# Feed-forward in eight blocks of 256 rows instead of four of 512: row-stationary gate and up, DMA transposes, queries in the first four units

## The chip, the cores and the metric

The kernel runs on one core of a Trainium2 chip. The metric is the device time of one launch in microseconds (us). Five engines matter: TensorE (PE in the profile, with its weight loads as PEld), VectorE (DVE), ScalarE (ACT), GpSimd (POOL) and SyncE, whose queue (SPq) issues nearly all DMAs.

## The reference

One transformer block on 2048 rows of width 512, with modulation vectors made from a condition `c`:

```python
x = A_x
mod = (_silu(c) @ w_mod).reshape(c.shape[0], 6, 1, -1)
sa, ca, ga, sb, cb, gb = (mod[:, 0], mod[:, 1], mod[:, 2], mod[:, 3], mod[:, 4], mod[:, 5])
h = _layernorm(x, axis=-1) * (1 + ca) + sa
x = x + ga * _A_ref(h, A_wq, A_wk, A_wv, A_wo)      # 32 heads of 16, one shared key and value head
h = _layernorm(x, axis=-1) * (1 + cb) + sb
x = x + gb * _B_ref(h, B_w_gate, B_w_up, B_w_down)  # (sigmoid(h Wg) * (h Wu)) Wd, inner width 1792
```

`_A_ref` is softmax attention over all 2048 keys. All inputs and the output are fp32.

## The kernel before

**Precision.** Every projection is made of three fp16 products: an fp32 operand is split into a high half and a low remainder, and high·high, low·high and high·low are added in PSUM. So each output tile of 128 rows and 512 columns costs three matmuls for every 128 of inner width.

**Attention.** The main loop runs over 32 units: eight query chunks of 256 rows (`NQ`), four groups of eight heads each (`NU`). A unit has 16 steps (`NKB`), one for each 128 keys. In a step PE makes four `sa` tiles (scores with queries on the partitions), whose row maxima DVE takes (`mx`), for units further on: these run 84 tiles ahead. It makes four `st` tiles (scores transposed, with the maximum already subtracted through extra rows of the query operand), which ACT turns into `P` by an exponential, and the products of `P` with `V` into the bank `craw`. At the end of a unit ACT copies `craw` into `cs`, a few small DMAs (`lD`, `raw`, `lc`) reorder it, and POOL makes the attention output `a` of that unit. All these matmuls use half the array's rows and a quarter of its columns each (64*32 in the profile); the helper `columns` issues four beside each other.

**Filling with feed-forward.** PE's spare time in each half step is filled by `piece`, which takes the next portion of a queue of groups: the query projections (`q`), the output projection (`wo`), gate and up (`gu`), down (`dn`). A `Couple` runs two groups on the upper and lower 64 rows of the array at once, so that one portion is eight 64*32 matmuls. `pick` chooses the next group, `places` spreads it over half steps at a rate (`RATE` 2.2 portions a half step, `QRATE` 0.55 for early queries, at most `MOST`). `pinned` order is kept: what the loop emits is each engine's program order.

**Blocks.** The feed-forward works on blocks of 512 rows (`QB`, four of them). When the eight units of a block are done, its four `wo` groups (128 rows each) are made in two Couples, then `norm`, `norm2` and `normed` (add to `x`, layer norm, on DVE and POOL), then PE transposes the normalised rows (`tr_part`, bank `pt`), and `split_evac` lets ACT scale and shift them and POOL split them into `h2h` and `h2l`, width on the partitions. For each of 14 chunks of 128 inner columns the weight chunk `gw` (512 KB, split halves kept in DRAM as `wD`) is stationary and the 512 rows of `h2` move: the gate bank goes through ACT (`th`, a tanh), the up bank through DVE (`u`), and POOL makes `gh` and `gl`, which already lie with inner width on the partitions, as `down_group` needs them.

**Tail.** The last block's attention ends with the loop, so its feed-forward runs alone, as full 128*128 matmuls (`alone`, line 187): the four down groups that `KEPT` left over, then transposes, 14 chunks of gate and up, and down.

**Weights** are loaded, scaled and split by `split_weight` during the first units (`WSTEPS`, `WLAST`); `w_down`'s first rows share their place with the query weights and come last. SP issues all DMAs from one queue in program order; a DMA there waits for its data and then the next one is reached. `defer(n, f)` emits `f` n steps later.

The lines with which the prediction works:

```python
def norm2(t, t1, xr):
    row_norm([t1], [xr], later=True)
    defer(1, lambda: normed(t, t1, xr))
...
gs += [Couple(gu_group(p, 0, at + p), gu_group(p, 1, at + p)) for p in range(max(lo, ahead), hi)]
gs += [Couple(down_group(t, lo), down_group(t + 1, lo)) for t in (0, 2)]
```

Of the kernel before, what the change touches and what calls it, by code (L numbers as in the profile page):

```python
# [16 lines left out]
P = 128  # L17
# [4 lines left out]
F = 1792  # L22
# [42 lines left out]
KEPT = 2  # L65
RATE = 2.2
QRATE = 0.55
ERATE = 1.2
AHEAD = 0, 0, 0, 0
MOST = 3  # L70
SWAP = 5
FRESH = 0.9
WSTEPS = 110
WLAST = 175
WLATE = 2
WSTORE = 5
FIRST = 140
# [7 lines left out]
GWB = 4  # L85
HBUFS = 36
# [3 lines left out]
def adaln_mqa_glu_kernel(  # L90
# [133 lines left out]
    def t16(name):  # L224
        return wp.tile([P, 512], F16, tag="f16", name=name, bufs=HBUFS)
# [76 lines left out]
    MCOLS = {1: ("ca", 1.0, SH), 0: ("sa", 0.0, SH), 4: ("sc", 1.0, SH), 3: ("sh", 0.0, SH)}  # L302
    MROWS = {2: ("ga", 1.0 / SW), 5: ("gb", 1.0 / (2.0 * SH * SW * SW))}

    def mod_end(i):
        p_ = mods[i]
        if i in MCOLS:
            name, add, mul = MCOLS[i]
            mods[i] = cp.tile([P, NDC], F32, name=name)
            dve.tensor_scalar(mods[i], p_[:, :NDC], add, mul, op0=ALU.add, op1=ALU.mult)  # L310
        else:
            name, scale = MROWS[i]
            mods[i] = cp.tile([P, D], F32, name=name)
            act.activation(mods[i], p_, AF.Identity, scale=scale)
# [38 lines left out]

    def split_evac(src, k, sc, sh, hi, lo):
        h32 = t32("h32")[:, :QU]
        act.activation(h32, src, AF.Identity, scale=sc[:, k:k + 1], bias=sh[:, k:k + 1])
        pool.tensor_scalar(hi, h32, 1.0, 0.0, op0=ALU.mult, op1=ALU.add)  # L357
        pool.tensor_tensor(lo, h32, hi, op=ALU.subtract)

# [93 lines left out]
    def ln1_high(b, k):  # L453
        hh, hl = h1.setdefault(b, ([], []))
        hh.append(t16(f"h1h{k}"))
        hl.append(t16(f"h1l{k}"))
        act.activation(hh[k], pts[b, k], AF.Identity, scale=mods[1][:, k:k + 1], bias=mods[0][:, k:k + 1])
# [24 lines left out]
    def k_high(b):  # L482
        pks[b, "h"] = kh = t16("kh")
        act.activation(kh, pks[b], AF.Identity, scale=kscale, bias=kbias)
# [22 lines left out]
    def q_group(b, o):  # L507
# [5 lines left out]
        def end(pq, second):  # L513
            qdone.add((b, o))
            q2 = wp.tile([P, 2, 512], F16, tag="q2", name="q2", bufs=2)
# [195 lines left out]
    def finish(b, o, raw):  # L711
        a_ = t16("a")
# [18 lines left out]
    def last_unit():  # L731
# [8 lines left out]
        a_ = t16("a")  # L740
# [14 lines left out]
    wD = dr.tile([NFC, P, 4, NDC, P], F16, name="wD")  # L755

    def gw_tile():
        return P2.tile([P, 4, NDC, P], F16, tag="gw", name="gw", bufs=GWB)

    def weight_jobs():
# [3 lines left out]
        def gate_up(f, m):  # L766
            if m == 0:
                gw[f] = gw_tile()
            split_weight((w_gate, w_up)[m][:, f * P:(f + 1) * P].rearrange("(k p) n -> p k n", p=P),
                         gw[f][:, 2 * m], gw[f][:, 2 * m + 1], [NDC, P],  # L770
                         (lambda: sp1.dma_start(wD[f], gw.pop(f))) if m == 1 else None)
# [3 lines left out]
        for f in [*range(4, NFC), *range(4)]:  # L775
            for m in range(2):
                jobs.append(lambda f=f, m=m: gate_up(f, m))
        for k in [*range(4, NFC), *range(4)]:
# [8 lines left out]
    class Transposes:  # L787
        stage, n = "tr", 4

        def __init__(self, part, u, sizes):  # L790
            self.part, self.u, self.sizes = part, u, sizes

        def alone(self):
            self.part(0, 4)

    def ffn_groups(b):
        x1 = {}
        xrs = {}
        h2 = {}
        gT = {}  # L800
        gws = {}
        ths = {}
        fs = [*range(4, NFC), *range(4)]
        HF = 8
        ahead = 2 * AHEAD[b]
        uses = [(p, 0) for p in range(ahead)]
        uses += [(p, None) for p in range(NFC)]
        asked = [0]

        def wo_group(t):  # L810
            def term(n, rs):
                o, i = divmod(n, 3)
                a_, w_ = passes(*aTs[2 * b + t // 2, o], WO['woh'], WO['wol'])[i]
                return a_[rs, t % 2 * P:(t % 2 + 1) * P], w_[rs, o, :]

            def begin():
                xrs[t] = t32("xr")
                sp1.dma_start(xrs[t], x[b * QB + t * P:b * QB + (t + 1) * P, :])

            def end(po, second):  # L820
# [6 lines left out]
                if tail:  # L827
                    dve.tensor_tensor(xr, t1, xr, op=ALU.add)
                    row_norm([t1], [xr])
                    normed(t, t1, xr)  # L830
                else:
                    defer(1 + 2 * (t % 2), lambda: norm(t, t1, xr))

            return Group("wo", 12, "po", term, end, begin)

# [9 lines left out]
        def normed(t, t1, xr):  # L845
            x1[t] = (xr, t1)
            if t % 2 == 1:
                marks[b, t // 2] = now[0]
            if t == (1 if ahead else 3):
                ask(2 if ahead else GWB - 1)  # L850

        pts2 = {}

        def tr_part(u, z, n0, n1):
            if n0 == 0:
                pts2[z] = bank("pt2")
            pt = pts2[z]
            for n in range(n0, n1):
                k, t = 2 * z + n // 2, 2 * u + n % 2
                pe.transpose(pt[:, n * P:(n + 1) * P], x1[t][1][:, k * P:(k + 1) * P], ident)  # L860
            if n1 == 4:
                for k in range(2 * z, 2 * z + 2):
                    if u == 0:
                        h2[k] = t16("h2h"), t16("h2l")
                    split_evac(pt[:, k % 2 * QU:(k % 2 + 1) * QU], k, mods[4], mods[3],
                               *(h_[:, u * QU:(u + 1) * QU] for h_ in h2[k]))

        def ask(upto):
            while asked[0] < min(upto, len(uses)):
                k = asked[0]  # L870
                gws[k] = gw_tile()
                sp1.dma_start(gws[k], wD[fs[uses[k][0]]])
                asked[0] += 1

        def parts_of(p):
            if p not in gT:
                gT[p] = t16("gh"), t16("gl")
            return gT[p]

        def gu_half(p, m, u, at):  # L880
            us = slice(u * QU, (u + 1) * QU)

            def term(n, rs):
                e, (k, i) = n // 12, divmod(n % 12, 3)
                gw = gws[at + e]
                w_, h_ = passes(gw[:, 2 * m], gw[:, 2 * m + 1], *h2[k])[i]
                return w_[rs, k, :], h_[rs, us], lambda z: z[:, e * QU:(e + 1) * QU]

            def end(p_, second):
                gated(p, m, p_, second, [(e, us, slice(e * QU, (e + 1) * QU)) for e in range(2)])  # L890

            return Group("gu", 24, "pgu", term, end, (lambda: ask(at + GWB)) if m == 0 else None, w=0.5)

        def gated(p, m, p_, second, pieces):
            if m == 0:
                ths[p] = th = t32("th")
                act.activation(th, p_, AF.Tanh, scale=0.5 / (SH * SW))  # L897
                return
            th = ths.pop(p)
            if second:  # L900
                u_ = t32("u")
                dve.tensor_copy(u_, p_)
                pool.tensor_scalar(th, th, 1.0, 1.0, op0=ALU.add, op1=ALU.mult)  # L903
                pool.tensor_tensor(th, th, u_, op=ALU.mult)
            else:
                dve.scalar_tensor_tensor(th, th, 1.0, p_, op0=ALU.add, op1=ALU.mult)  # L906
            for e, to, of in pieces:
                hi, lo = parts_of(fs[p + e])
                pool.tensor_scalar(hi[:, to], th[:, of], 1.0, 0.0, op0=ALU.mult, op1=ALU.add)
                pool.tensor_tensor(lo[:, to], th[:, of], hi[:, to], op=ALU.subtract)  # L910

        def gu_group(p, m, at):
            def term(n, rs):
                k, i = divmod(n, 3)
                gw = gws[at]
                w_, h_ = passes(gw[:, 2 * m], gw[:, 2 * m + 1], *h2[k])[i]
                return w_[rs, k, :], h_[rs]

            def end(p_, second):
                gated(p, m, p_, second, [(0, slice(0, QB), slice(0, QB))])  # L920

            return Group("gu", 12, "pgu", term, end, (lambda: ask(at + GWB)) if m == 0 else None)

        def down_group(t, lo):
            n_ = HF if lo == 0 else NFC - HF

            def term(n, rs):
                f, i = fs[lo + n // 3], n % 3
                g_, w_ = passes(*gT[f], wdh, wdl)[i]
                return g_[rs, t * P:(t + 1) * P], w_[rs, f, :]  # L930

            def end(p_, second):
# [8 lines left out]
                else:  # L941
                    pool.tensor_tensor(ot, ot, x1[t][0], op=ALU.add)
                    store = lambda: sp1.dma_start(out[b * QB + t * P:b * QB + (t + 1) * P, :], ot)
                    if tail:
                        store()
                    else:
                        defer(2 + t % 2, store)
# [3 lines left out]
        wos = [wo_group(t) for t in range(4)]  # L951
        trs = [Transposes(lambda n0, n1, u=u, z=z: tr_part(u, z, n0, n1), u, ([4], [4, 0])[z]) for z in range(2) for u in range(2)]
        gs = []
        at = len(uses) - NFC
        es = [Couple(gu_half(p, 0, 0, p), gu_half(p, 1, 0, p)) for p in range(0, ahead, 2)]
        gs += [Couple(gu_half(p, 0, 1, at + p), gu_half(p, 1, 1, at + p)) for p in range(0, ahead, 2)]
        for lo, hi in ((0, HF), (HF, NFC)):
# [263 lines left out]
```

## Time and profile before

| | |
|---|---|
| median of 3 runs | 1664.54 us (1663.61 to 1665.8) |
| span of the profiled execution | 1661.5 us |
| mean granted TensorE clock | 0.994 |
| PE / DVE / ACT / POOL busy, share of the span | 98% / 85% / 78% / 38% |
| DMA | 94.06 MB, mean 57 GB/s |
| first copy of `craw` (unit 0 ends) / last (unit 31 ends) | 153.4 / 1524.4 us |

The profiled execution's own time is its span of 1661.5 us and the launch around it; the median of the timed runs stands 3.0 us above that span. Units can be told apart in the trace by ACT's 32 copies `cs<-craw`, one at the end of each. A matmul's duration in the profile includes the way through the array, so 379 ns stands beside starts that are 0.22 us apart; rates are read from starts, or from counts over a stretch, not from durations.

### The profile page before, as it was taken

Reading aid. Unit: us, or ns where it says so; the run is one execution under the profiler, and the core shown is the slowest. Engines: PE = TensorE matmul, PEld = TensorE weight load, DVE = VectorE, ACT = ScalarE, POOL = GpSimd, SP = SyncE. Lnnn points to the kernel's source line nnn. Section 1 sums busy time; section 2 is a strip of 40 time slices with the busy share of each in tenths; the row PEclk is TensorE's granted clock in tenths of the full one; section 3 lists DMA queues with packets and bytes.
Section 4 is the critical chain, followed back from the end, with each engine's and each line's share of the span. In section 5 each row is a group of like instructions: output and inputs, shape, how many; then the busy total and the mean of one; then the engine's idle time right before and its main releaser. Section 6 shows DMA issues by size and latency. Waiting matters only on the chain.

```text
span 1661.5 us, 87862 instructions
## 1 busy us (share of the span) xinstructions
PE 1621.0 (98%) x39688; PEld 960.2 (58%) x39688; DVE 1417.0 (85%) x2396; ACT 1292.8 (78%) x2335; POOL 623.6 (38%) x818
## 2 busy tenths in 40 slices
PE   6899999999999999999999999999999999999998
PEld 3334444454456666666666667666667666654443
DVE  7889999999999999999999999999999999921211
ACT  5548999989888888888888888888888888884100
POOL 5432455466033342223552231233543323232423
PEclk9979999999999999999999999999999999999999
DMA  7121333331011120111121110101121101111211
GB/s 241 63 63 30 102 117 98 98 96 41 21 58 50 53 71 16 41 29 29 41 79 54 38 41 15 37 27 28 41 79 54 54 28 29 37 49 46 83 51 39
DMA packets 86723, 94.06 MB, mean 57 GB/s; under 512 B 24916, under 2 KB 65868, under 8 KB 86348
## 3 DMA queue, kind: packets, MB, share of 16 engines
q1 hardware_dynamic: 86348, 88.44, 16.9%
q8 instruction: 311, 5.10, 1.3%
q14 instruction: 64, 0.52, 0.1%
HBM read 67.82 MB, written 16.24 MB: 51 GB/s over the span
## 4 chain that ended last, share of the span: by engine, by line
PE 85%; DVE 9%; ACT 3%; issue 1%; DMA 1%; SPq 1%; POOL 0%; POOLq 0%; ACTq 0%; DVEq 0%
PE craw L136 24%; PE sa L136 17%; PE pgu L136 15%; PE st L136 10%; DVE mx L136 7%; PE pd L136 6%; PE pgu L187 4%; PE pd L187 3%; PE po L136 2%; PE pq L136 2%; ACT P L136 1%; DMA xall<-in_A_x_dram 1%; DVE st L136 1%; ACT h L136 1%; ACT th L136 0%
## 5 line engine op out<-in xcount | busy, mean ns | idle before, releaser
L136 DVE TENSOR_REDUCE mx<-sa 128x1 f32<-128x512 f32 x2048 | 1295.5, 682 | 60.2 <-PE sa L136 26.9
L136 ACT ACTIVATE P<-st 128x512 f32<-128x512 f32 x2048 | 1172.4, 597 | 186.3 <-PE st L136 125.1
L136 PE MATMUL craw<-P,V 64*32 64x512 f32 x8192 | 1086.1, 597 | 0.3 <-ACT cs L136 0.3
L136 PE MATMUL st<-qp,kp 64*32 64x512 f16 x8192 | 828.6, 379 | 8.2 <-ACT P L136 7.6
L136 PE MATMUL sa<-kp,qp 64*32 64x512 f16 (+1 forms) x7940 | 823.1, 378 | 7.5 <-DVE mx L136 7.1
L136 PEld LDWEIGHTS <-kp 64*32 64x32 f16 x8192 | 326.6, 91 | 281.6 <-issue 130.5
L136 PEld LDWEIGHTS <-qp 64*32 64x32 f16 (+1 forms) x7940 | 276.4, 92 | 145.0 <-issue 60.2
L136 PE MATMUL pgu<-h2h,gw 64*32 64x512 f16 x5376 | 273.9, 376 | 1.8 <-ACT th L136 0.4
L136 PEld LDWEIGHTS <-gw 64*32 64x32 f16 x8064 | 173.3, 92 | 65.4 <-issue 16.4
L136 PEld LDWEIGHTS craw<-P,V 64*32 64x32 f32 x8192 | 186.7, 105 | 16.5 <-issue 1.6
L903 POOL TENSOR_SCALAR th<-th 128x512 f32<-128x512 f32 x42 | 26.0, 619 | 392.1 <-ACT th L136 300.2
L136 PE MATMUL pgu<-h2l,gw 64*32 64x512 f16 x2688 | 164.2, 376 | 0.0
L322 POOL TENSOR_SCALAR wst<-wst 128x512 f32<-128x512 f32 x46 | 28.6, 621 | 136.4 <-DMA wst<-in_B_w_up_dram 91.7
L897 ACT ACTIVATE th<-pgu 128x512 f32<-128x512 f32 x14 | 8.4, 597 | 82.2 <-PE pgu L187 82.2
L558 POOL MEMSET qp<- 32x1024 f16 x60 | 56.7, 945 | 41.6 <-PE st L136 38.8
L136 PE MATMUL pd<-wdh,gh 64*32 64x512 f16 x1152 | 69.5, 376 | 0.4
L136 PE MATMUL pd<-wdl,gh 64*32 64x512 f16 x1152 | 69.6, 376 | 0.0
L136 PE MATMUL pd<-wdh,gl 64*32 64x512 f16 x1152 | 69.3, 376 | 0.0
L136 DVE COPY u<-pgu 128x512 f32<-128x512 f32 x42 | 28.6, 682 | 46.6 <-PE pgu L136 27.0
L187 PE MATMUL pgu<-h2h,gw 128*128 128x512 f16 x224 | 66.9, 379 | 1.2 <-POOL h2h L357 1.2
L910 POOL TENSOR_TENSOR gl<-th,gh 128x512 f16<-128x512 f32 x56 | 65.1, 1163 | 4.7
L906 DVE SCALAR_TENSOR_TENSOR th<-th,pgu 128x512 f32<-128x512 f32 x14 | 9.6, 688 | 66.6 <-PE pgu L187 51.8
(159 smaller groups left out, 1412.7 us busy)
## 6 DMA issues: line engine op xcount, KB each, us to landing
gw<-wD SPq DMA_DIRECT2D x56, 512.0 KB
wD<-gw SPq DMA_DIRECT2D x14, 512.0 KB
wm<-in_w_mod_dram SPq DMA_DIRECT2D x6, 1024.0 KB
qp<-qD SPq DMA_DIRECT2D x192, 32.0 KB
qD<-q SPq DMA_DIRECT2D x16, 256.0 KB
xr<-in_A_x_dram SPq DMA_DIRECT2D x16, 256.0 KB
out_dram<-ot SPq DMA_DIRECT2D x16, 256.0 KB
raw<-cs SPq DMA_DIRECT2D x248, 16.0 KB
```

Source lines behind the costliest of these rows:

```text
L136: return (lambda *a, **k: keep(f_(*a, **k))) if pinned else f_
L187: pe.matmul(cut[0](self.bank) if cut else self.bank, l_, r_, start=(n == 0), stop=(n == self.n - 1))
L322: pool.tensor_scalar(w_, w_, SW, 0.0, op0=ALU.mult, op1=ALU.add)
L558: eng.memset(qp[j:j + 32], 0.0)
L897: act.activation(th, p_, AF.Tanh, scale=0.5 / (SH * SW))
L903: pool.tensor_scalar(th, th, 1.0, 1.0, op0=ALU.add, op1=ALU.mult)
L906: dve.scalar_tensor_tensor(th, th, 1.0, p_, op0=ALU.add, op1=ALU.mult)
L910: pool.tensor_tensor(lo[:, to], th[:, of], hi[:, to], op=ALU.subtract)
```

## The change

- **Blocks of 256 rows.** `ffn_block(b)` replaces `ffn_groups(b)`: there is one for each query chunk of four units, eight in all. Seven run inside the loop, the eighth in the tail. `pick` takes a block's `wo` from `urgent` at step 9 after its attention ended, and everything else from `work`, whose groups name in `needs` the transposes that they wait for. `pace` sets the rate so that a block's work is done by step 26 (`CHAIN`) of the period after next.
- **Rows stationary.** In the loop `gu_group(c_, t)` takes 128 rows of `h2` as the stationary operand and moves 512 weight columns, 256 of gate and 256 of up. There are seven chunks of 256 inner columns; a chunk `gw` is 1 MB, and two buffers hold them (`GWB` 2, before four of 512 KB). The bank then holds gate and up of the same rows: ACT makes a tanh of the first half of both tiles and a copy of one second half, DVE copies the other. POOL's four operations in `gated_rows` are as many and as large as before for the same numbers.
- **Transposes by DMA.** Since rows now lie on the partitions, the gated values (`gr` to `g`) and the normalised rows (`h2r` to `h2`) are turned by `dma_start_transpose` on SP: each turns 128 rows by 1024 fp16 values (256 KB). There are nine in a block of the loop, 63 in all. The step `norm3` is new: POOL multiplies by the scale, adds the shift and splits the rows before that. The PE transposes of the loop (48) and `split_evac` are gone.
- **Tail.** The last block (256 rows) keeps weights stationary (`gu_cols`), moves 256 columns, and transposes on PE (`turn_rows`).
- **Queries.** All query projections are issued in units 0 to 3, at `QRATE` 1.1; before, they reached into unit 7. Weight splitting ends earlier (`WSTEPS` 90, `WLAST` 100).

```diff
-KEPT = 2
-RATE = 2.2
-QRATE = 0.55
+CHAIN = 26
+QRATE = 1.1
 MOST = 3
+LEAST = 2.0
+HELD = 60
-WSTEPS = 110
-WLAST = 175
+WSTEPS = 90
+WLAST = 100
+HLATE = 3
+GLATE = 3
-GWB = 4
-HBUFS = 36
+GWB = 2
+HBUFS = 18
...
-    wD = dr.tile([NFC, P, 4, NDC, P], F16, name="wD")
+    wD = dr.tile([NCH, P, NDC, 4, 256], F16, name="wD")
...
         def norm2(t, t1, xr):
             row_norm([t1], [xr], later=True)
-            defer(1, lambda: normed(t, t1, xr))
+            defer(1, lambda: norm3(t, t1, xr))
+
+        def norm3(t, t1, xr):
+            x1[t] = xr, t1
+            pool.tensor_tensor(t1, t1, mods[4], op=ALU.mult)
+            pool.tensor_tensor(t1, t1, mods[3], op=ALU.add)
+            rows = pair("h2r")
+            pool.tensor_scalar(rows[:, 0], t1, 1.0, 0.0, op0=ALU.mult, op1=ALU.add)
+            pool.tensor_tensor(rows[:, 1], t1, rows[:, 0], op=ALU.subtract)
+            h2[t] = turned(rows, f"h2{t}")
+            if b == 0 and t == 0:
+                ask(0)
+            defer(HLATE, h2[t][1])
+
+        def turned(rows, name):
+            t_ = pair(name).rearrange("p a (c r) -> p (a c) r", r=P)
+
+            def go():
+                sp1.dma_start_transpose(t_, rows.rearrange("p a n -> p (a n)"))
+                marks[b, name] = now[0]
+
+            return t_, go
...
-        def gu_group(p, m, at):
+        def gu_group(c_, t):
...
             def term(n, rs):
                 k, i = divmod(n, 3)
-                gw = gws[at]
-                w_, h_ = passes(gw[:, 2 * m], gw[:, 2 * m + 1], *h2[k])[i]
-                return w_[rs, k, :], h_[rs]
+                gw = gws[at + c_]
+                h_, w_ = ((0, 0), (1, 0), (0, 1))[i]
+                return h2[t][0][rs, 4 * h_ + k, :], gw[rs, k, 2 * w_:2 * w_ + 2, :].rearrange("p m n -> p (m n)")
 
             def end(p_, second):
-                gated(p, m, p_, second, [(0, slice(0, QB), slice(0, QB))])
+                ts = slice(256 * t, 256 * (t + 1))
+                th, u_ = ths[c_], ups[c_]
+                if second:
+                    dve.tensor_copy(u_[:, ts], p_[:, 256:])
+                    act.activation(th[:, ts], p_[:, :256], AF.Tanh, scale=0.5 / (SH * SW))
+                else:
+                    act.activation(th[:, ts], p_[:, :256], AF.Tanh, scale=0.5 / (SH * SW))
+                    act.activation(u_[:, ts], p_[:, 256:], AF.Identity)
+                if t == 1:
+                    gated_rows(c_)
...
     def pick(s):
...
+        if urgent and s >= urgent[0].ready:
+            return urgent.pop(0)
+        if work and all(k in marks and s >= marks[k] + GAP for k in getattr(work[0], "needs", ())):
+            return work.pop(0)
...
-        if o == 0 and b % 2 == 1 and b < NQ - 1:
-            blocks[b // 2] = ffn_groups(b // 2)
...
+        if o == 0 and b > 0:
+            first_, rest = ffn_block(b - 1)
+            first_.ready = i * NKB + SKIP
+            urgent.append(first_)
+            work.extend(rest)
```

Three places of the built program show what moved.

SP's queue where one block of the loop ends and the next begins (the second such turn after the change; `qp` are the queries of a coming unit, `mh` its maxima, `lD`, `lc` and `raw` the reordering of `cs`). Before:

```order
L136 DMA raw<-cs 16x256 x8
L136 DMA lc<-lD 128x16
L136 DMA qp<-qD 16x4x256 x6
L136 DMA lD<-rc 128x16
L136 DMA raw<-lD 128x1x256
L136 DMA out_dram<-ot 128x512
L136 DMA xr<-in_A_x_dram 128x512 x2
L136 DMA out_dram<-ot 128x512
L136 DMA qp<-mh 1x16x64 x4
```

Now:

```order
L139 DMA raw<-cs 16x256 x8
L139 DMA lc<-lD 128x16
L139 DMA qp<-qD 16x4x256 x6
L139 DMA lD<-rc 128x16
L139 DMA_TRANSPOSE h_14182<-h2r 128x8x128
L139 DMA raw<-lD 128x1x256
L139 DMA_TRANSPOSE h_14396<-h2r 128x8x128
L139 DMA out_dram<-ot 128x512 x2
L139 DMA gw<-wD 128x4096
L139 DMA qp<-mh 1x16x64 x4
```

The two transposes of the normalised rows stand ahead of the stores of the block before, of the next weight chunk and of the maxima's rows.

ACT's program at the end of a gate and up group in the middle of the loop (the `P` rows are the exponentials). Before:

```order
L136 ACTIVATE P_28450<-st 128x512
L136 ACTIVATE P_28467<-st 128x512
L136 ACTIVATE th<-pgu 128x512
L136 ACTIVATE P_28506<-st 128x512
L136 ACTIVATE P_28524<-st 128x512
```

Now:

```order
L139 ACTIVATE P_24430<-st 128x512
L139 ACTIVATE P_24447<-st 128x512
L139 ACTIVATE th<-pgu 128x256
L139 ACTIVATE u<-pgu 128x256
L139 ACTIVATE th<-pgu 128x256
L139 ACTIVATE P_24486<-st 128x512
L139 ACTIVATE P_24504<-st 128x512
```

Three operations of 256 columns stand between two exponentials where one of 512 stood.

PE's program in the tail, where the transposes end and gate and up begin. Before:

```order
L860 MATMUL pt_48093<-ident,t_47978 128x128
L860 MATMUL pt_48093<-ident,t_47959 128x128
L860 MATMUL pt_48093<-ident,t_47978 128x128
L187 LDWEIGHTS gw
L187 MATMUL pgu<-h2h,gw 128x512
```

Now:

```order
L967 MATMUL pt_50156<-ident,t_50081 128x128
L967 MATMUL pt_50156<-ident,t_50060 128x128
L967 MATMUL pt_50156<-ident,t_50081 128x128
L190 LDWEIGHTS gw
L190 MATMUL pgu<-h2c,gw 128x256
```

There are 336 such matmuls in the tail before and after; each now moves 256 columns. The matmuls of the down projection in the tail go from 240 to 168.

Counted in the built program, the 64*32 matmuls of queries, output projection, gate, up and down in the loop go from 13,824 to 15,744. By units they are: before, 136 to 144 in most of units 0 to 4, 288 in unit 5, 384 in units 6 to 8 together, 11,376 in units 9 to 29 and 1,104 in units 30 and 31; after, 248, 264, 256, 192, 192 and 224 in units 0 to 5, 1,648 in units 6 to 8, 11,568 in units 9 to 29 and 1,152 in units 30 and 31.

More of the change, by code (lines that the diff above doesn't have):

```diff
@@ L889, in end @@
             def end(p_, second):
[L890 to L910, printed above, removed]
@@ L1181, in adaln_mqa_glu_kernel @@
     last_unit()
-    left = [*spare, *[z[1] for z in main if z[0] is not None]]
+    left = [*urgent, *work]
     for g in left[:1]:
```

307 lines of the change are left out of this document (152 added, 155 removed).

## The prediction

> **What bounds the kernel now.** I read the busy shares first, then cut the span into stages at the ends of units and asked each stage for its busy times and its number of `cs` copies (one for each unit), and then the order of PE inside a half step, the tail in the chain that ended last, and the timelines of POOL, PE and SP where a block turns. The page's 40 slices:
>
> ```profile
> PE   6899999999999999999999999999999999999998
> DVE  7889999999999999999999999999999999921211
> ```
>
> PE looks full throughout, DVE until the tail. Stages, with us, then busy us and instructions of PE, PEld, DVE, ACT, POOL; below them the same stages with `cs` alone:
>
> ```profile
> 195.80:318.40 122.60, 120.56 (x2770) 59.41 (x2763) 119.28 (x204) 111.12 (x206) 60.86 (x78) 1.00 0.33 101
> 361.20:485.30 124.10, 121.78 (x2715) 59.07 (x2702) 121.03 (x211) 111.61 (x209) 45.18 (x65) 1.00 0.12 34
> 485.30:1434.10 948.80, 942.88 (x27879) 628.63 (x27879) 909.61 (x1503) 821.14 (x1479) 335.80 (x423) 1.00 0.14 43
> 1434.10:1525.20 91.10, 90.03 (x2237) 49.94 (x2221) 28.44 (x47) 72.44 (x131) 25.68 (x30) 1.00 0.16 50
> 1525.20:1661.50 136.30, 129.73 (x606) 60.05 (x606) 27.20 (x47) 12.61 (x23) 49.15 (x58) 1.00 0.16 55
> ...
> 195.80:318.40 122.60, 0.00 (x0) 0.00 (x0) 1.79 (x3) 1.00 0.33 101
> 361.20:485.30 124.10, 0.00 (x0) 0.00 (x0) 1.79 (x3) 1.00 0.12 34
> 485.30:1434.10 948.80, 0.00 (x0) 0.00 (x0) 12.53 (x21) 1.00 0.14 43
> ```
>
> Units 2 to 4 and 6 to 8 take 40.9 and 41.4 us, with DVE 97 to 98% busy; units 9 to 29, full of feed-forward, 45.2, with DVE at 96% and PE at 99%. The clock is 1.00 in all. So there are two bounds, and PE's own starts tell them apart:
>
> ```profile
> 1282.13 0.46 PE L136 MATMUL pgu<-h2h,gw 64*32 64x512 f16 x8
> 1282.35 0.46 PE L136 MATMUL pgu<-h2l,gw 64*32 64x512 f16 x8
> 1282.57 0.41 PE L136 MATMUL sa<-kp,qp 64*32 64x512 f16 x4
> 1282.63 0.62 PE L136 MATMUL craw<-P,V 64*32 64x512 f32 x4
> 1282.78 0.41 PE L136 MATMUL st<-qp,kp 64*32 64x512 f16 x4
> ...
> 1283.43 0.68 PE L136 MATMUL pgu<-h2h,gw 64*32 64x512 f16 x16
> ...
> 807.24 6.03 DVE L136 TENSOR_REDUCE mx<-sa 128x1 f32<-128x512 f32 x10
> ```
>
> A portion of eight feed-forward matmuls takes 0.22 us; attention's share of a half step runs from 1282.57 to 1283.43, 0.86 us. A unit has 32 half steps, 27.5 us, so attention alone leaves PE free for 13 us of DVE's unit: 64 maxima at 0.60 are 38.6 us. With 542 feed-forward matmuls a unit (11,376 in 21), 68 portions or 14.6 us, PE comes to 42.1 of 45.2; the other 3.1 are unit turns and bank hand-overs, which I keep. Up to some 400 matmuls a unit are covered by DVE; what exceeds that costs 0.22 us for eight. Units 2 to 8 hold far less, and the tail is PE alone:
>
> ```profile
> 1527.09 7.77 PE pd L187 x36
> 1534.86 1.29 PE po L187 x6
> 1536.15 7.78 PE pd L187 x36
> ...
> 1548.88 40.09 PE pgu L187 x185
> ...
> 1609.69 31.08 PE pgu L187 x144
> 1640.77 11.67 PE pd L187 x54
> ```
>
> There a matmul of 512 columns costs 0.216 us (31.08 / 144).
>
> **The sum, part by part,** against this execution's span.
>
> Units 0 to 5 get 416 more matmuls (52 portions, 11.2 us of PE). At up to 264 a unit PE needs 27.5 + 3.1 + 7.1 = 37.7, under DVE's 40.9, so DVE covers the queries. Unit 5's last seven steps carry the first gate and up work at the full rate, 45.2 / 16 = 2.82 a step for 2.55: 1.9; with the queries' evictions coming twice as often I take +3 (0 to 11).
>
> Units 6 to 8 leave the DVE bound for the full rate: 3 x 45.2 = 135.6 for 124.1, +11.5.
>
> Units 9 to 29 get 192 more, 24 portions, +5.2. They lose the PE transposes and ACT's evictions of them, and get ACT's bursts instead:
>
> ```profile
> 816.61 0.63 PE L136 MATMUL pt<-ident,t 128*128 128x128 f32 x4 [0.21 <-DVE ot L136]
> ...
> L136 ACT ACTIVATE th<-pgu 128x512 f32<-128x512 f32 x42 | 24.8, 592 | 0.1
> L136 ACT ACTIVATE h<-pt,sh,sc 128x256 f32<-128x256 f32 x24 | 12.4, 581 | 0.0
> ...
> 1529.45 0.42 ACT L744 ACTIVATE a<-raw 128x256 f16<-128x256 f32 x1 [4.41 <-DVE raw L743]
> ```
>
> Twelve fours of transposes at 0.63 are 7.6 us off PE. At a group's end ACT now does three pieces of 0.42 before the next exponential for one of 0.59: 0.67 us more, about 37 times. ACT is idle 13% of such a step, 0.37 us, and PE runs two `st` banks ahead, so most of it is absorbed; unabsorbed it would be 25. I take a quarter, +6. DVE's copy halves and covers nothing new. Together +3.6 (-2 to +23).
>
> Units 30 and 31: 48 more matmuls, +1.3.
>
> The tail loses half of gate and up and 72 down matmuls. The price of a 256-column matmul with its own weight load is not in the trace; it lies between half of 0.216, if the load hides, and 0.216, if it doesn't.
>
> ```profile
> 77.56 0.17 PE L136 MATMUL pv<-wkvh,h1l 128*128 128x16 f16 x1
> ...
> 77.79 0.17 PE L136 MATMUL pv<-wkvh,h1l 128*128 128x16 f16 x1
> ...
> L187 PEld LDWEIGHTS <-gw 128*128 128x128 f16 x336 | 32.8, 98 | 41.3 <-issue 2.1
> ```
>
> The nearest rows: ten starts from 77.56 to 77.79, each with a load of 128x128 in front, stand 25.6 ns apart, though one load takes 98 ns by itself. So loads run ahead, and I take 0.108. The Trainium skill ("TensorE: Matmul & The Clock Gate", LDWEIGHTS) prices a load at columns / 1.2, 107 ns for 128; added to the matmul as a serial cost that would give 336 x 0.215 = 72 us, no gain on gate and up, and a total of 1671. The 25.6 ns rows speak against that here.
>
> So gate and up: 336 x (0.216 - 0.108) = -36.3; down of the last block 84 for 168, -18.1; of the block before, 84 are left over for 72, +2.6. The norm chain grows by four DVE operations on 128x512, some 2.5 us (four of the 0.6 us that a maximum takes), and the gap from 1543.93 to 1548.88 that hides transposes and evictions shrinks by half the transposes; +1.5 for both (0 to 6). A wait for the last chunk's split, +0.5. The loads:
>
> ```profile
> 847.13 5.65 SPq L136 DMA_DIRECT2D raw<-cs  x8
> ...
> 1574.00:1579.00 5.00, 5.00 (x25) 2.25 (x24) 0.51 (x2) 0.60 (x1) 1.78 (x2) 1.00 0.30 105
> ```
>
> In 5 us of the tail the DMA engines are 0.30 busy and move 105 GB/s, 525 KB, one old chunk: 1.5 us for 512 KB. A new chunk of 1 MB needs 3.0, and PE works 48 x 0.108 = 5.2 on the one before; covered. Tail: -49.8.
>
> The DMA transposes are the price that no row shows. What must hold is the time between POOL's last split and PE's first use of `h2`:
>
> ```profile
> 803.42 2.09 POOL L352 TENSOR_SCALAR t<-xr,mv,rs 128x512 f32<-128x512 f32 x1
> 806.42 0.69 DVE L136 BATCH_NORM_STATS2 st<-xr 128x6 f32<-128x512 f32 x1
> 807.41 0.23 POOL L340 TENSOR_SCALAR ve<-mv 128x1 f32<-128x1 f32 x1 [1.89 <-DVE mv L136]
> 809.50 2.10 POOL L352 TENSOR_SCALAR t<-xr,mv,rs 128x512 f32<-128x512 f32 x1
> ...
> 795.12 1.28 POOL L824 TENSOR_TENSOR t<-t,ga 128x512 f32<-128x512 f32 x1
> ...
> L909 POOL TENSOR_SCALAR gh<-th 128x512 f16<-128x512 f32 x56 | 34.8, 621 | 46.9 <-DVE th L906 43.2
> L910 POOL TENSOR_TENSOR gl<-th,gh 128x512 f16<-128x512 f32 x56 | 65.1, 1163 | 4.7
> ```
>
> `norm3` adds 2 x 1.28 + 0.62 + 1.16 = 4.4 us of POOL for each of two tiles. The first ends its norm at 805.5, so its `norm3` would end at 809.9; the second's norm of 4.2 us (807.4 to 811.6 now) then ends at 814.1, its `norm3` at 818.5. PE is to begin six steps after the second tile's statistics (806.4): one to `norm3`, three of `HLATE`, two of `GAP`. Four filled steps at 2.82 and two unfilled at 2.55 are 16.4: 822.8. So a transpose that lands within 4.3 us of its issue costs nothing. Low end: a plain transfer of 256 KB, half of the 1.5 us, and an issue of 5.65 / 8 = 0.71. High end: one issue for each block of 16 rows by 128 columns, 64 x 0.71 = 45 us. I take about 4, nearest to eight column blocks or less, since it is the same number of bytes in one instruction: 0 on the sum. SP is held by it while `qp`, `raw`, `gw` stand behind; a chunk `gw` is asked for a whole couple (24 portions, some 15 us) ahead, so it can bear that. The gated values have the other block's `wo` between them and the down group that needs the last of them.
>
> Sum: +3 + 11.5 + 3.6 + 1.3 - 49.8 = -30.4, so 1661.5 - 30.4 = 1631.1; the median stood 3.0 above the span, and I expect the same: 1634.
>
> **The rivals.**
>
> 1. Slower: the transposes. If one takes T from issue to landing, PE stalls T - 4.3 at the head of each of seven blocks. At T = 8.6 the gain of 30 is gone; that is the point from which it decides. At 14 us it gives 1634 + 7 x 9.7 = 1702. For it: no row has such a transfer, and SP takes 0.71 us for each of eight DMAs of 16 KB. Against: two steps stand between issue and use, and a plain 256 KB moves in 0.75. The Trainium skill ("DMA: Bandwidth & Descriptors", Latency and other measured facts) gives DMA transposes 261 GB/s, 1.0 us for 256 KB by that estimate, which no run here shows.
> 2. Slower: 256-column matmuls cost as much as 512-column ones; 1634 + 36 = 1670. Against: the 25.6 ns rows.
> 3. Less gain: ACT's bursts reach PE in full (+19) and the first units take the whole price of their portions (+8): 1661, on the edge of no change. For it: ACT is 87% busy in units 9 to 29.
>
> **How the numbers follow.** A measurement of this kernel tells 0.2%, 3.3 us, from no change. The forecast with its own terms (1620 to 1648) gets 0.60. Rival 1 beyond T = 8.6 gets 0.14; between 4.3 and 8.6, 1634 to 1664, 0.08. Rival 2 gets 0.05, rival 3 and halves of it 0.13. Faster: 0.60 + 0.07 + 0.11 = 0.78; same 0.03; slower 0.14 + 0.05 = 0.19. Below 1616 I leave 0.05, above 1676 most of rival 1: range 1616 to 1676.
>
> **What would show it.** The last `cs` at about 1544 for 1524; units 6 to 8 at 45 us each; the tail at 87 us with `pgu` starts 0.108 apart; no idle PE at the first `pgu` of each block. PE waiting for `h2` or `g`, or SP rows of many us for the transposes, would show rival 1; `pgu` starts 0.2 apart, rival 2; units 9 to 29 at 46 or more with PE released by ACT's `P`, rival 3. The forecast is wrong if any of these is there.

## The result and the profile after

The changed kernel takes 1683.34 us (median of 4 runs, 1679.56 to 1685.34), the kernel before, run beside it, 1665.17. The ratio is 1.0099 (95% interval 1.0079 to 1.0119): 18 us slower by the medians, where the forecast was 30 us faster. The profiled execution has a span of 1680.5 us. Cut at the `cs` copies, as in the prediction:

| us | units 0 to 5 | 6 to 8 | 9 to 29 | 30, 31 | tail | span |
|---|---|---|---|---|---|---|
| before | 360.5 | 124.1 | 948.7 | 91.1 | 137.0 | 1661.5 |
| after | 382.6 | 138.7 | 975.3 | 96.1 | 87.8 | 1680.5 |
| difference | +22.1 | +14.6 | +26.6 | +5.0 | -49.2 | +19.0 |
| forecast | +3 | +11.5 | +3.6 | +1.3 | -49.8 | -30.4 |

The tail did what was expected. Everything that is wrong lies in the loop: +68 us for the +19 of the forecast. The stages of the kernel after, units 2 to 4 first (us; busy us and instructions of PE, PEld, DVE, ACT, POOL; clock, DMA share, GB/s):

```profile
197.10:327.30 130.20, 123.81 (x2976) 63.51 (x2959) 120.41 (x206) 113.23 (x209) 78.28 (x98) 0.99 0.36 115
382.60:521.30 138.70, 136.63 (x3989) 90.05 (x3979) 128.18 (x212) 118.70 (x222) 46.38 (x55) 1.00 0.32 77
521.30:1496.60 975.30, 954.48 (x27998) 628.10 (x27985) 906.97 (x1505) 826.35 (x1533) 363.75 (x426) 1.00 0.29 72
```

In units 9 to 29 neither PE nor DVE is as full as before (98% and 93% for 99% and 96%), so no engine has become the bound; they wait more. The DMA share has doubled, 0.29 for 0.14. The waits of PE, with us in total, times and the longest (last, the only wait for "issue" in the loop of the kernel before):

```profile
PE pgu L139 <- DMA h<-h2r: 11.4, 3, 9.4
PE st L139 <- ACT P L139: 7.2, 15, 0.9
PE pgu L139 <- issue: 7.0, 8, 1.9
PE sa L139 <- DVE mx L139: 5.5, 13, 1.4
PE st L139 <- issue: 4.0, 4, 2.1
PE sa L139 <- issue: 2.9, 3, 1.5
PE po L139 <- POOL a L720: 2.5, 1, 2.5
PE pgu L190 <- DMA gw<-wD: 1.8, 1, 1.8
PE craw L139 <- issue: 1.2, 2, 0.9
...
PE pgu L136 <- issue: 0.2, 1, 0.2
```

Waits for `P` and `mx` are no longer than before (7.6 and 7.1 there). New are one long wait for the transposed rows, one for `a`, and 17 waits for "issue", 15 us, in which PE waited for no data that the profile shows; before there was one, of 0.2 us.

**The tail.** `pgu` has become two runs of 256-column matmuls:

```profile
1617.63 10.66 PE L190 MATMUL pgu<-h2c,gw 128*128 128x256 f16 x96
1630.05 15.18 PE L190 MATMUL pgu<-h2c,gw 128*128 128x256 f16 x137 [1.76 <-DMA gw<-wD]
```

96 in 10.66 us are 0.111 each: the load of the weights, 98 ns by itself, hides here.

**The first block.** SP's queue, three pieces of POOL's work and PE at the step where gate and up of the first block begin:

```profile
343.05 1.36 SPq L139 DMA_TRANSPOSE h<-h2r  x1
346.45 0.36 SPq L139 DMA_DIRECT2D lD<-rc  x1
355.71 1.24 SPq L139 DMA_TRANSPOSE h<-h2r  x1
...
344.23 0.62 POOL L333 TENSOR_SCALAR wst<-wst 128x512 f32<-128x512 f32 x1
346.88 0.23 POOL L351 TENSOR_SCALAR ve<-mv 128x1 f32<-128x1 f32 x1
354.53 1.15 POOL L852 TENSOR_TENSOR h2r<-t,h2r 128x512 f16<-128x512 f32 x1
...
358.77 1.04 PE L139 MATMUL pgu<-gw,h 64*32 64x512 f16 x12 [9.38 <-DMA h<-h2r]
```

The first tile's rows are turned at 343.05. POOL then splits weights (L333 to L335), makes the second tile's norm from 346.88 and its split until 355.68; SP stands before that transpose for 9 us, PE from 349.39 to 358.77. In the six later blocks 13.0 us pass from the second tile's statistics on DVE to the issue of its transpose, in this one 22.0. The transpose itself is short. Over all 63, the last packet lands 3.3 us (median) after SP reaches the issue, 2.6 at least, and 5.3 to 7.1 for the six where a chunk `gw` went just ahead.

**"Issue".** PE's stop at 629 us, and the DMA queues in the 6.3 us ahead of it and in the 3.8 us after (queue: packets, MB, share of 16 engines):

```profile
628.68 0.55 PE L139 MATMUL pgu<-gw,h 64*32 64x512 f16 x7
631.13 0.40 PE L139 MATMUL pgu<-gw,h 64*32 64x512 f16 x5 [1.90 <-issue]
...
622.31 0.53 SPq L139 DMA_DIRECT2D gw<-wD  x1
622.94 1.51 SPq L139 DMA_TRANSPOSE g<-gr  x1
625.13 3.42 SPq L139 DMA_DIRECT2D qp<-qD  x6
...
q1 hardware_dynamic: 903, 1.25, 73.5%
...
q1 hardware_dynamic: 956, 0.28, 90.0%
q8 instruction: 1, 0.02, 1.9%
```

What matters is what is missing: queue q8, which brings instructions in packets of 16 KB, has no packet in 6.3 us, while q1 moves a chunk and a transpose. Units 6 to 29 hold 250 such packets and 63,917 matmuls and weight loads, 256 for each packet, so these are PE's instructions; their median distance is 4.2 us. By the packets of the trace one starts at 620.91 and the next at 628.26, 7.4 later and 0.5 after the chunk's last packet; it ends at 629.42, and PE starts again 1.7 us after that. From unit 6 to 29 PE has 16 gaps over 0.4 us, 17.0 us in all. The profile puts two of them down to the transposed rows (2.0 us), one to `P` and 13 to "issue" (13.8 us). Of the 13, 12 follow a packet that came 6.2 to 7.4 us after the one before, and all end 1.2 to 1.7 us after a packet's end. In the same units of the kernel before there are six gaps, 3.9 us, all before `st` and released by `P`.

A long distance is not enough by itself. In these units of the changed kernel 17 packets came over 6.3 us after the one before, and 11 of them were followed by such a wait for "issue". In the kernel before there are 19, 11 of them in units 6 to 8, where there is little feed-forward, and no wait for "issue" above 0.2 us.

**Steps.** A step is the time from one step's first `P` to the next's. In both kernels the undisturbed ones take about 2.65 us with four portions in them, 2.87 with five, then 3.08, 3.30, 3.51. What the portions alone would make of units 9 to 29, what the steps at a couple's end take above that, and all others:

| us, units 9 to 29 | portions | couples' ends | other | sum |
|---|---|---|---|---|
| before | 915.0 | 8.7 | 24.8 | 948.5 |
| after | 920.8 | 23.9 | 29.8 | 974.5 |
| after, chunks not loaded (below) | 920.8 | 18.8 | 14.6 | 954.2 |
| before, chunks loaded twice (below) | 915.0 | 12.8 | 34.8 | 962.6 |

### The profile page after: what moved, and what is told of

It is laid out like the page before. It is cut to its first block, busy times and chain, and to the rows that moved or that the text cites. A ratio compares the mean times of both kernels' runs of the same rounds, so it can differ in the third digit from the quotient of the medians.

```text
span 1680.5 us, 91637 instructions
## 1 busy us (share of the span) xinstructions
PE 1608.2 (96%) x41477; PEld 991.0 (59%) x41477; DVE 1419.8 (84%) x2400; ACT 1305.5 (78%) x2409; POOL 666.2 (40%) x827
## 4 chain that ended last, share of the span: by engine, by line
PE 81%; POOL 5%; ACT 4%; DVE 4%; DMA 3%; issue 2%; SPq 2%; POOLq 0%; ACTq 0%
PE craw L139 22%; PE pgu L139 17%; PE sa L139 16%; PE st L139 9%; PE pd L139 7%; PE po L139 3%; PE pgu L190 2%; PE pd L190 2%; PE pq L139 2%; DVE mx L139 2%; ACT P L139 2%; SPq L139 1%; POOL t L363 1%; DMA h<-h2r 1%; DMA xall<-in_A_x_dram 1%
## 5 line engine op out<-in xcount | busy, mean ns | idle before, releaser
L139 PE MATMUL pgu<-gw,h 64*32 64x512 f16 x9408 | 422.2, 378 | 21.9 <-DMA h<-h2r 11.4
L139 PEld LDWEIGHTS <-h 64*32 64x32 f16 (+1 forms) x9600 | 211.8, 92 | 107.0 <-issue 41.7
L139 PE MATMUL pd<-wdh,g 64*32 64x512 f16 x2688 | 132.8, 377 | 0.8
L139 PEld LDWEIGHTS <-g 64*32 64x32 f16 x4032 | 86.7, 92 | 33.9 <-issue 6.7
L139 PE MATMUL pd<-wdl,g 64*32 64x512 f16 x1344 | 80.1, 376 | 0.0
L896 POOL TENSOR_TENSOR th<-th,u 128x512 f32<-128x512 f32 x49 | 62.9, 1284 | 4.1
L333 POOL TENSOR_SCALAR wst<-wst 128x512 f32<-128x512 f32 x46 | 28.4, 618 | 86.3 <-DMA wst<-in_B_w_gate_dram 28.8
L139 DVE COPY u<-pgu 128x256 f32<-128x256 f32 x49 | 20.3, 415 | 49.8 <-PE pgu L139 22.5
L899 POOL TENSOR_TENSOR gr<-th,gr 128x512 f16<-128x512 f32 x49 | 57.1, 1164 | 4.0
L139 PE MATMUL craw<-nought 64*32 64x1 f16 x353 | 57.8, 164 | 0.0
L139 PE MATMUL pq<-h,wdh 64*32 64x512 f16 (+1 forms) x688 | 53.8, 386 | 0.1
```

The source lines that it names most:

```text
L139: return (lambda *a, **k: keep(f_(*a, **k))) if pinned else f_
L333: pool.tensor_scalar(w_, w_, SW, 0.0, op0=ALU.mult, op1=ALU.add)
L899: pool.tensor_tensor(rows[:, 1], th, rows[:, 0], op=ALU.subtract)
```

## Experiments

The theory from this profile had three parts: POOL is late in the first block (some 16 us); PE's instructions come late behind the 1 MB chunks (some 20 us); ACT's burst of small evictions at a couple's end (some 15 us). Times stand beside the kernel before on the same chip, so ratios are compared; the changed kernel's is 1.0099. Two of the runs compute wrong values: the one without chunk loads uses old weights, and the one with plain transfers leaves the values unturned.

**Halves.** `sp1.dma_start(gws[k], wD[c])` becomes two:

```diff
+sp1.dma_start(gws[k][:, :2], wD[c][:, :2])
+defer(1, lambda: sp1.dma_start(gws[k][:, 2:], wD[c][:, 2:]))
```

> The changed kernel with each 1 MB chunk of gate and up weights loaded in two 512 KB halves, the second one step later. Theory (late instructions): PE's instruction fetches (16 KB each, one about every 4.3 us while feed-forward runs) stand behind a whole 1 MB chunk, so that some come 6.3 to 7.6 us after the one before, and PE stands still 0.5 to 2 us about 16 times; in halves a fetch waits 1.5 us at most: those gaps go, 12 to 20 us less, 1664 to 1672 us. Rival (transposes): it is the DMA transposes' many small packets, not the chunks, that hold the fetches up: less than 4 us change. Rival (late weights): the second half comes too late for its matmuls: slower.

1684.7 us, ratio 1.0111 (1.0087 to 1.0135): no gain. 15 gaps were left, and packets of instructions still came up to 7.7 us apart. At 1229 to 1239 us of that run a second half followed the first after 1.7 us, with two loads of `xr` right behind, and the engines were 14/16 busy for over 4 us with no packet of q8. So this run did not tell the theories apart; one step was too close there.

**Both copies of u on DVE, or both on ACT.**

```diff
-act.activation(u_[:, ts], p_[:, 256:], AF.Identity)
+dve.tensor_copy(u_[:, ts], p_[:, 256:])
```

> The changed kernel with both copies of u on DVE, so that ACT has two pieces of 0.42 us at a couple's end and DVE two of 0.415. Theory (ACT burst): steps with a couple's end take 0.50 to 0.65 us over their portions because ACT's three pieces come on top of four exponentials of 0.60 (3.65 us for a step of 2.65); with two pieces ACT and DVE both need 3.25, so about 0.35 us goes from each of 49 ends: 8 to 17 us less, 1667 to 1675. Rival (DVE takes over): the second copy puts DVE, at 2.42 us of maxima a step, over its step and the maxima late: no gain, 0 to +8 us. Rival (the ends aren't what costs): within 3 us.

> The changed kernel with both copies of u on ACT: the suspected cost made larger, four ACT pieces of 0.42 us at a couple's end and none on DVE. Theory (ACT burst): every piece beyond ACT's slack is passed on in full, 0.42 us at each of 49 ends: 16 to 21 us more, 1699 to 1705. Rival (DVE or the banks set the end, ACT has slack): within 5 us of the changed kernel, or faster by what DVE's copies cost.

On DVE: 1705.61 us, 1.0230 (1.0215 to 1.0245), 22 us worse. On ACT: 1685.71, 1.0119 (1.0102 to 1.0136), not to be told from the changed kernel. Both expectations of the ACT theory failed, and the loss on DVE was larger than any rival had it. One end in the changed kernel (first five rows) and in the run with both on DVE (the others):

```profile
882.02 0.38 ACT L139 ACTIVATE th<-pgu 128x256 f32<-128x256 f32 x1
882.29 0.39 ACT L139 ACTIVATE u<-pgu 128x256 f32<-128x256 f32 x1
882.55 0.41 ACT L139 ACTIVATE th<-pgu 128x256 f32<-128x256 f32 x1
882.81 1.12 ACT L139 ACTIVATE P<-st 128x512 f32<-128x512 f32 x2
882.08 0.40 DVE L139 COPY u<-pgu 128x256 f32<-128x256 f32 x1
...
886.50 0.38 ACT L139 ACTIVATE th<-pgu 128x256 f32<-128x256 f32 x1
887.76 0.38 ACT L139 ACTIVATE th<-pgu 128x256 f32<-128x256 f32 x1 [0.88 <-DVE u L139]
888.04 1.08 ACT L139 ACTIVATE P<-st 128x512 f32<-128x512 f32 x2
886.97 0.76 DVE L139 COPY u<-pgu 128x256 f32<-128x256 f32 x2 [0.33 <-issue]
```

With both on DVE the two engines take turns in this trace: each bank holds `th`'s and `u`'s source, and the second to read it begins when the first has ended. So ACT idles 0.88 us, and its next exponential comes 1.54 us after the first `th` for 0.79. A step with an end has an excess of 0.24 (median) before, 0.64 after, 1.21 with both on DVE and 0.78 with both on ACT. ACT's third and fourth piece are not passed on in full: 0.4 us more on ACT, with 0.4 off DVE, cost 0.14. How the changed kernel's 0.40 over before divides between ACT's burst and the next couple's wait for the banks stays open.

**POOL's splits early, the first block later.** `WSTEPS = WLAST = 72`, and in `pick`:

```diff
-s >= marks[k] + GAP
+s >= marks[k] + GAP + 4 * (k[0] == 0)
```

> The changed kernel with the weight splits of POOL finished by step 72 (the last four from step 72 on) where they ran to step 109. Theory (POOL in the first block): the step of 6.4 us in unit 4 (wo waits for POOL's a) and the one of 14.7 us in unit 5 (gate and up wait for the second tile's transpose, issued at 355.7 because POOL split weights between the pieces of its norm) go: 15.7 us less minus what the splits cost earlier (up to 4), 1667 to 1672. Rival (the chain itself): norm, split and transpose are that long for the first block without the splits: less than 5 us change.

> The changed kernel with nothing but the first block's gate and up begun four steps later. If the 12.0 us step in unit 5 is PE standing in front of rows that POOL has not yet finished, attention goes on instead, and most of it goes: 8 to 11 us less (four steps' feed-forward is to be made good later), 1672 to 1676 us. If PE stood there for the chunk or for a bank: no change.

> The changed kernel with POOL's splits finished from step 72 on and the first block's gate and up four steps later, chunks loaded whole. If the parts add: 1683 - 7.6 - 5.5 = 1670 (1667 to 1673). The run with quarters besides took 1659; if that is so, quarters are worth 8 to 12 us here, though only 3.4 by themselves, and PE's gaps behind late fetches are more and longer here than with quarters. If this run takes 1659 too, the quarters were worth nothing.

Early: 1675.75, 1.0055 (1.0036 to 1.0075). Later: 1675.08, 1.0046 (1.0031 to 1.0062). Both: 1673.51, 1.0036 (1.0023 to 1.0050). The early splits gave less than expected, the two together just missed their range. Unit 5's wait for `h` shrinks from 9.4 to 5.2 us with the early splits and to 0.4 with the later begin, and units 0 to 5 go from 382.6 to 373.0, 370.4 and 366.1 us. In the last two, units 6 to 8 go from 138.7 to 143.4 and 143.9. The 14 portions made good there are worth 3.0 us; I had put them at 2. The rest is in PE's waits: three gaps of 0.3 to 1.6 us in each run, and none in the run with quarters besides (below), where the stage takes 138.2. The stall in unit 5 is POOL's lateness, and it's cheaper to let attention go on than to stand before the rows. The splits are only part of that lateness: with early splits still 17.8 us pass from the second tile's statistics to the issue of its transpose, for 22.0 with late ones and 13.0 in later blocks. Three pieces of a last split (2.4 us) and a clearing of `qp` (1.9 us) still stand on POOL between 324 and 329 us, around the start of the first tile's norm. The second tile's rows then come 8.9 us after the first's, as in every later block.

**Chunks not loaded, chunks loaded twice.** In the first, `gws[k] = gws[k - 2]` from the third chunk of the loop on. In the second, the kernel before gets a second load behind each:

```diff
 sp1.dma_start(gws[k], wD[fs[uses[k][0]]])
+if not tail:
+    sp1.dma_start(again, wD[fs[uses[k][0]]])
```

> The changed kernel with only the first two chunks and the tail's loaded; in between the two tiles are used again and again, so the values are wrong (48 MB less to load). Theory (late instructions): without the chunks no fetch of PE's instructions is late by more than a transpose or an xr: 14 to 22 us less, 1661 to 1669 us. Rival (the chunks cost nothing): within 4 us of 1683.

> The kernel before, with every load of a 512 KB chunk followed by a second load of the same chunk into a spare tile that nothing reads (until the tail): the feed-forward weights' traffic of the changed kernel, 1 MB at a time, without any other part of the change. Theory (PE's instruction fetches stand behind long runs of queued data): gaps of 0.5 to 2 us in PE behind fetches over 5.3 us apart appear in units 9 to 29, where there are almost none now, 8 to 20 us more, 1675 to 1687 us. Rival (the gaps come from something else in the changed kernel, the turned rows or the 256-row blocks' order): within 4 us of 1667.

Not loaded: 1656.74, 0.9935 (0.9920 to 0.9950), 27 us less than the changed kernel, more than expected. Its PE has no wait for "issue" but one of 0.2 us, and in units 6 to 29 one gap over 0.4 for 16, before the transposed rows. Loaded twice: 1678.73, 1.0057 (1.0037 to 1.0078), 11 us slower than before though nothing reads the second copy. Bytes from HBM in before, after, without loads and with double loads, and then PE's wait for "issue" without loads and those with double loads:

```profile
HBM read 67.82 MB, written 16.24 MB: 51 GB/s over the span
...
HBM read 97.18 MB, written 16.24 MB: 67 GB/s over the span
...
HBM read 46.85 MB, written 16.24 MB: 38 GB/s over the span
...
HBM read 89.84 MB, written 16.24 MB: 63 GB/s over the span
...
PE sa L139 <- issue: 0.2, 1, 0.2
...
PE pgu L136 <- issue: 6.3, 8, 1.3
PE craw L136 <- issue: 1.6, 1, 1.6
PE st L136 <- issue: 0.9, 1, 0.9
PE sa L136 <- issue: 0.3, 1, 0.3
```

With 22 MB more to load, the kernel before gets ten gaps released by "issue" (8.8 us) where it had none; those released by `P` stay about as they were (seven, 5.0 us, for six, 3.9 us). So the loads cause the waits for "issue"; that was shown in both directions. It is not that SP's queue is held and comes late: in the loop of both kernels and of the run with double loads no matmul waits for a chunk or for `qp`. Nor is it all idle time: of the 20.4 us that units 9 to 29 lose to the loads in the changed kernel, PE's idle time makes 14.6 (20.8 for 6.2), and the other 5.8 are in its busy time at the same number of matmuls, which no run takes apart. That a late packet of instructions is the link was not varied by itself: it rests on their times, and on the profile naming no other wait. The Trainium skill ("Runtime: NRT & Kernel Launch", Instruction fetch mechanics) says that an engine's instructions come in 16 KiB blocks by a DMA queue of its own and that this is mostly hidden. The trace agrees with the blocks, about 1 us each; here they are not always hidden when one comes over 6.3 us after the one before.

**Quarters, and plain transfers for the transposes.** Four loads of 256 KB, one step apart; and, by itself, `dma_start` in the place of `dma_start_transpose`.

> The changed kernel with each 1 MB chunk loaded in four pieces of 256 KB, one step apart. With halves one step apart the fetches of PE's instructions still came up to 7.6 us apart, since a second half, an xr or a transpose stood right behind the first and the DMA engines stayed 14/16 busy for 4 to 5 us. Theory (late instructions, behind any long run of queued data): pieces of 0.8 us leave the engines free between them, a fetch waits 1 us at most where no other transfer joins: 8 to 18 us less, 1665 to 1675 us. Rival (fetches late for another reason than queued data): less than 4 us change, fetches still over 6.3 us apart in feed-forward.

> The changed kernel with each DMA transpose replaced by a plain transfer of the same 256 KB between the same tiles (the values are not turned, so the result is wrong). Theory (any queued data counts, a transpose by its 2 us of the engines): 2 to 6 us less. Rival (the many small packets of the transposes are what holds fetches and other transfers up): 10 to 20 us less, no fetch over 6.3 us apart. If SP's 1.25 us for a transpose's issue mattered, it would show as gw, qp and raw issued earlier.

Quarters 1679.93, 1.0068 (1.0048 to 1.0088); plain 1679.61, 1.0068 too. Both intervals touch the changed kernel's, so each gain of some 5 us is uncertain, and that of quarters is less than expected. With quarters the gaps in units 6 to 29 shrink to 11.7 us, plain to 11.5. The transposes' small packets are not the main thing: with plain transfers packets of instructions still came over 6.3 us apart 16 times there, for 17 in the changed kernel and 9 with quarters.

**All that helped.**

> Three changes together: quarters one step apart, POOL's splits finished from step 72 on, and the first block's gate and up begun four steps later (step 92 for 88), so that PE does attention alone until the second tile's transpose has landed. The splits alone gave 7.6 us; the later begin should take the 7.8 us of the step in unit 5 that was left, less about 2 for denser units 6 to 9: 1683 - 7.6 - 5.5 = 1670; with the quarters' 8 to 18 us 1652 to 1662, under the kernel before's 1666. If quarters give nothing: 1668 to 1672. If the wait in unit 5 isn't on the transposed rows, the later begin gives nothing: 1675.

> The version with early splits and the later first block again, now with three chunk buffers for two, each chunk asked for two couples ahead instead of one and loaded in quarters two steps apart (one step apart before). Theory (late instructions): quarters that follow each other after some 5 us can't queue up behind one another, so that a fetch meets one piece of 0.8 us and at most a transpose or an xr: of the some 6 us of gaps and the steps drawn out beside them that were left with quarters one step apart, 3 to 6 us go: 1653 to 1657 us. Floor by the run without chunk loads: it took 26.6 us less than the changed kernel, which would make 1647 here. Rival (what is left is no longer the loads): 1657 to 1661.

Early splits, later begin and quarters: 1659.13 us (median of 10), 0.9953 (0.9938 to 0.9968). It beats both kernels, the changed one by 1.5% and the one before by 0.5%. What is left of the new waits of PE:

```profile
PE pgu L139 <- issue: 3.1, 6, 0.7
PE pgu L139 <- DMA h<-h2r: 1.5, 1, 1.5
PE st L139 <- issue: 1.4, 1, 1.4
PE craw L139 <- issue: 0.6, 1, 0.6
```

Against whole chunks (1.0036) quarters are worth 14 us here, though some 5 by themselves. Why the two parts don't add was not shown; the later begin moves all packets of instructions against all transfers, so that others may meet. The third buffer, with chunks asked two couples ahead and quarters two steps apart, missed: 1664.59, 0.9984 (0.9969 to 0.9999). Units 9 to 29 are faster (964.0 for 967.5 us), but units 6 to 8 go from 138.2 to 144.8. Its first block asks for the second and third chunk together, the second chunk's last quarter comes six steps later, and PE stands before it:

```profile
382.21 0.41 PE L139 MATMUL pgu<-gw,h 64*32 64x512 f16 x8 [2.83 <-DMA gw<-wD]
```

## Why the prediction was wrong, point by point

- **The tail, -49.8: right** (-49.2), with 0.111 us for a matmul of 256 columns where 0.108 was taken. Rival 2 fell. "Covered" was wrong for the chunk loaded at the tail's head: 1.8 us. These two make 2.8 us more than forecast, so the other terms came out some 2 us smaller; that they nearly cancel is luck.
- **Units 6 to 8, +11.5: right for the work.** The portions alone come to +11.4; the other 3.2 are chunk loads: without them the stage takes 135.3 us for the forecast's 135.6.
- **The transposes, 0 provided that they land within 4.3 us: right on the transfer**, 2.6 to 4.2 us for all but six, and PE stands before `h` for 9.4 us in the first block and 2.0 in the six others together. Rival 1 fell. **The step that failed is the lead of 4.3 us (`norm3` ends at 818.5, PE begins at 822.8), read in a later block and taken for all seven.** In the later blocks its 12.1 us from the second tile's statistics to the end of `norm3` come to 13.0, in the first to 22.0. There POOL still splits weights, as the new `WSTEPS` itself says. The two steps where PE stands take 15.7 us more than an undisturbed one: 12.0 in unit 5 and 3.7 in unit 4, where `wo` waits for POOL's `a`. With early splits the two still take 9.8 more, so the splits are not the whole of it.
- **Units 9 to 29, +3.6: wrong, +26.6.** Of its terms, +5.2 for portions was right (+5.8). -7.6 for the PE transposes gone is not contradicted: the column "other" falls by 10.2 when no chunks are loaded, which also takes out what the old loads cost. +6 for ACT's bursts was too small, +10.1 by the column of ends without chunk loads, though ACT's part in it was not shown alone; rival 3 had 25, 19 more than the 6. **The term that is missing is the loads: "a chunk `gw` is asked for a whole couple (24 portions, some 15 us) ahead, so it can bear that" asked whether a chunk comes in time for its matmuls.** It does: in the loop each is issued 8.3 us or more ahead of its first matmul. What was not asked is what a chunk holds up meanwhile. Blocks of half as many rows read every weight twice as often, 29 MB more, and the forecast had no term for that. Loading costs 27 us, 20.4 of them in these units. That is for all 50 MB that the run without loads leaves out, so a part of it was in the kernel before already, where 22 MB more cost 11 us.
- **Units 0 to 5, +3:** besides the 15.7 there are 6.4, 4.9 of them in units 0 to 3. The upper end of the term, 11, holds that.
- **Units 30 and 31, +1.3:** +5.0. 0.8 goes without the loads; the portions alone make +2.5.

The sum: of the loop's +68 us, 20 are portions (0.3, 11.4, 5.8 and 2.5 by stage), 2 more than the forecast's 18. The other 48 are stalls and longer ends of couples, net of the transposes gone, which it had at about 1; the tail's 49 don't pay for both. The signs named for a wrong forecast were there: idle PE at the first block's `pgu`, and units over 46 us, but with PE released by "issue" and not by `P`. None of the rivals had the loads or POOL's splits as a cause.

## What to carry to other kernels

A transfer that arrives in time for its own reader can still cost. Here it cost 11 to 27 us, most likely because PE's next instructions came behind it. When a smaller block makes an operand be read twice as often, price the extra bytes by what they hold up, and try loading in pieces with time between them, beside the other fixes: quarters gave some 5 us alone and 14 with two others. When a step moves to an engine, look at that engine in the first block as well as in a settled one.

## What was not expected of the hardware

After some of its gaps PE ran at half its clock. Stretches with the granted clock third from the end: in the changed kernel the 2 us after the gap of 9.38 us, 2 us after the gap of 2.49 us that ends at 308.47, then 2 us about a gap of 2.09 us and the stretch behind; last, in the run with halves, a gap of 1.98 us and the stretch behind:

```profile
358.80:361.00 2.20, 2.20 (x40) 1.05 (x48) 0.69 (x1) 0.60 (x1) 0.80 (x2) 0.50 0.99 319
...
310.00:312.00 2.00, 2.00 (x41) 1.02 (x33) 1.72 (x4) 0.86 (x2) 1.60 (x3) 0.50 0.01 2
...
821.40:823.40 2.00, 0.00 (x0) 0.00 (x0) 0.69 (x1) 0.11 (x1) 0.09 (x1) 1.00 1.17 128
823.50:825.50 2.00, 2.00 (x73) 1.26 (x80) 0.80 (x2) 1.25 (x3) 1.62 (x3) 1.00 0.04 8
...
1369.10:1371.00 1.90, 0.00 (x0) 0.00 (x0) 0.67 (x1) 0.68 (x2) 0.00 (x0) 1.00 0.32 38
1371.30:1374.70 3.40, 3.40 (x63) 1.84 (x55) 1.82 (x4) 2.02 (x5) 1.50 (x2) 0.50 0.09 17
```

The step with the wait of 9.4 us took 12.0 us more than an undisturbed one. After that wait the clock is 0.50 until 364.0; by an estimate from these rows the 5.2 us at half the clock lose 2.6, which with the wait makes the 12.0. The wait of 2.5 us cost 3.7. A gap's length alone doesn't decide: gaps of 1.98 us (halves) and 1.87 (early splits) were followed by 3.4 us at 0.50, gaps of 2.09 and 1.90 in the changed kernel by none. In all runs every gap of 2.3 us or more in the loop was followed by it. The Trainium skill ("TensorE: Matmul & The Clock Gate", Part 1: The HAM clock gate) puts the fall to half the clock after an idle window of some 3.4 us; here gaps of 1.9 to 2.5 us were followed by it. Second, a transpose of 256 KB holds SP for 1.2 to 2.7 us at its issue, where a plain load of a 1 MB chunk holds it for 0.3 to 0.6 mostly.
